# Block maxima by transposing reductions, and the last turn of the mixing beside its product with U

## The chip, the cores and the metric

The kernel runs on one core of a Trainium2 chip. The metric is the device time of one launch in microseconds (us). TensorE (PE) does matrix products and turns (a product with the identity), VectorE (DVE) and ScalarE (ACT) read the products' banks in PSUM, GpSimd (POOL) and SyncE (SP) do the rest. Each engine works through its own queue in order.

## The reference

Three stages on 8 batches, 576 positions, 8 heads of 64 columns:

```python
scores = scale * np.matmul(q, k.transpose(0, 1, 3, 2))
scores = np.where(block_i >= block_j, scores, -1000000000.0)   # blocks of 64
scores = scores - np.max(scores, axis=-1, keepdims=True)
attn = np.exp(scores)
attn = attn / (np.sum(attn, axis=-1, keepdims=True) + 1e-09)
x = np.matmul(attn, v)                       # heads side by side: 576 x 512
...
h = x.transpose(0, 2, 1) @ U @ V             # U: 576 x 32, V: 32 x 576
u = x + h.transpose(0, 2, 1)
x = u + np.maximum(u @ w_ch1, 0.0) @ w_ch2   # 512 -> 2048 -> 512
...
gate = 1.0 / (1.0 + np.exp(-gate_pre))       # causal convolution of 5 steps
out = gate * (x @ w_val) @ w_out
```

## The kernel before

**Stages.** Up to about 240 us PE does the attention of the first two batches (16 heads, "units", queries on the partitions) and the first MLP steps, while 32 conversion steps split the MLP's weights into a high and a low part (DMA, ACT's `magnitude` at L120, four DVE operations at L122 to L143, a cast on ACT). From there to about 1060 us it does the MLP, three products per tile so that a high and a low part together give full precision (`h` at L964, `acc` at L1016), and lays the attention of the other 48 heads between these products. Then come the convolution, the gate and the last two products.

**What sets the order.** PE's order is written by hand: a generator yields pieces of attention and mixing, and the MLP calls `gap()` after a few products, which takes the next piece. What a piece issues on DVE, ACT and POOL is put in its place in their queues by a scheduler, by its own reckoning of when it is ready. In the units (`slot`) the mixing's steps are run to their end with no other PE work within (`for _ in step(pn): pass`). In the late heads (`tick`, `mixing`) each `yield` lets some MLP products in between, six in the places spoken of below.

**Late heads.** Scores of a head lie keys by queries, as five tiles in two halves of 832 and 768 columns (`s`, in places called `za` and `zb`). The softmax's maximum runs over keys, that is over partitions and tiles: `emit_max_a` takes the maximum of the tiles by four operations (L609, L611), `emit_max_b` transposes the result in blocks of 32 by 32 (L618, L619) and takes the maximum in each block's row (L621, 18 columns), and `emit_max_c` joins the four groups of 32 partitions and spreads the result back (`mb`). DVE subtracts it (L647), ACT takes the exponential (L671), PE multiplies by the values (`emit_pv`). `emit_norm_a` turns the row of sums (`lt`) onto the partitions (L745), adds 1e-9 (L747) and takes the reciprocal, and POOL multiplies.

**Mixing.** For each pair of heads (32 pairs: 8 in the units, 24 late) three steps follow each other: `mix_T` turns the head output `xt` in five turns of 128, 128, 128, 128 and 64 positions and splits it into high and low (ACT's cast at L91, DVE's subtraction at L97) in `x`, a buffer that there is once; `mix_G` multiplies by U (five products at L811 into the bank `pG`, 256 columns wide) and adds high and low (L813, L814); `mix_H` multiplies by V (L834) and adds to `xt`. The fifth turn (L803) has a bank of its own. `mix_G` of a pair comes two or more pieces behind its `mix_T`.

**Where the banks come from.** `pT`, `pG`, `pH`, `pPV` and the score pieces take turns in the same pool of PSUM banks (`ps_p`, tag "a"), so a piece that takes one waits for what was last evicted from it.

Of the kernel before, what the change touches and what calls it, by code (L numbers as in the profile page):

```python
# [8 lines left out]
F32 = mybir.dt.float32  # L9
# [4 lines left out]
ALU = mybir.AluOpType  # L14
AX = mybir.AxisListType
PSUM = bass.MemoryType.PSUM
DRAM = bass.MemoryType.DRAM
P = 128
# [4 lines left out]
def attn_moe_gate_kernel(ctx: ExitStack, tc: tile.TileContext, q, k, v, U, V, w1, w2, wval, convw, wout, out):  # L23
# [59 lines left out]
    NB32 = S // 32  # L83

    def f32(ap):
        return ap if ap.dtype == F32 else ap.bitcast(F32)

    vec, act, pool, pe, sp = nc.vector, nc.scalar, nc.gpsimd, nc.tensor, nc.sync

    def hi_act(o, i):  # L90
        act.copy(o, i)  # L91
# [4 lines left out]
    def lo(eng, o, i, h):  # L96
        eng.tensor_tensor(o, i, f32(h), op=ALU.subtract)  # L97
# [9 lines left out]
    def noted(at, ins):  # L107

        mark[at] = ins.ins

    def behind(at):

        return tc.issue_after(mark[at]) if at in mark else nullcontext()
# [77 lines left out]
    def rpool(name, bufs):  # L191
        return att.enter_context(tc.tile_pool(name=name, bufs=bufs, side="right"))
# [8 lines left out]
    tiny_p = rpool("tinyp", 2)  # L201
    ps_p = att.enter_context(tc.tile_pool(name="psp", bufs=ABUF, space=PSUM, side="right"))
# [17 lines left out]
    ident = ac_p.tile([P, P], F32, name="ident")  # L220
# [15 lines left out]
    NTT = (S + P - 1) // P  # L236
    tok = [(P * i, min(P, S - P * i)) for i in range(NTT)]

    def rot(tag, bufs=2, dtype=F32, n=S):
        return rot_p.tile([P, n], dtype, tag=tag, bufs=bufs, name=tag)  # L240
# [46 lines left out]
    NK = NTT  # L287
    q0 = [P * j for j in range(NK)]
    wid = [S - q0[j] for j in range(NK)]
    parts = [(4, 3, 0), (1, 2)]  # L290
    soff, half_of = {}, {}
    sw = []
    for h, js in enumerate(parts):
        o = 0
# [104 lines left out]
    stt = {}  # L399
# [153 lines left out]
    def slot(u):  # L553
# [32 lines left out]
        for step, delay in ((mix_H2, 6), (mix_G, 5), (mix_T, 4)):  # L586
            pn, off = divmod(u - delay, 2)
            if off == 0 and 0 <= pn < 2 * NP:
                with tc.high_priority() if pn == NP - 1 else ExitStack():
                    for _ in step(pn):  # L590
                        pass
                yield False
# [8 lines left out]
    def sv(n, j, a=0):  # L601
        return stt[n][half_of[j]][:, soff[j] + a:soff[j] + wid[j]]

    mbt = {}
    mxt = {}

    def emit_max_a(n):
        m = rot("m", 1)
        vec.tensor_tensor(m[:, P:], sv(n, 0, P), sv(n, 1), op=ALU.max)  # L609
        for j in range(2, NK):  # L610
            x = vec.tensor_tensor(m[:, q0[j]:], m[:, q0[j]:], sv(n, j), op=ALU.max)  # L611
        noted(1, x)
        mxt[n] = m

    def emit_max_b(n):
        m = mxt.pop(n)
        t = rot("t")
        vec.transpose(t[:, 0:P], sv(n, 0)[:, 0:P])  # L618
        vec.transpose(t[:, P:], m[:, P:])  # L619
        r = tiny_p.tile([P, NB32], F32, tag="r0", name="r0")  # L620
        vec.reduce_max(r, t.rearrange("p (j a) -> p j a", a=32), axis=AX.X)  # L621
        mxt[n] = r

    def emit_max_c(n):
# [69 lines left out]
    xts = {}  # L694
# [45 lines left out]

    def emit_norm_a(pn):
        lt = lts.pop(pn)
        t = rot("t")
        with behind(NR0 if pn < NP else 0):
            vec.transpose(t, lt)  # L745
        r = tiny_p.tile([P, NB32], F32, tag="r0", name="r0")
        vec.tensor_scalar(r, t.rearrange("p (j a) -> p j a", a=32)[:, :, 0], 1e-9, None, op0=ALU.add)  # L747
        vec.reciprocal(r, r)
        nrm[pn] = r

# [8 lines left out]
    gst = {}  # L759
# [25 lines left out]
    def mix_T(pn):  # L785
        xt = xts[pn]
        full = S // P
        if not xfix:
            xfix.append(rot("x", 1, F32R, NTT * 2 * P).rearrange("p (i c m) -> p i c m", c=2, m=P))
            pool.memset(f32(xfix[0][tok[-1][1]:, NTT - 1]), 0.0)  # L790
        x = xfix[0]
        gst[pn] = x
        ps = ps_p.tile([P, 512], F32, tag="a", name="pT")
        for i in range(full):
            pe.transpose(ps[:, i * P:(i + 1) * P], xt[:, i * P:(i + 1) * P], ident)  # L795
        pv = ps[:, 0:full * P].rearrange("p (i m) -> p i m", m=P)
        hi_act(x[:, 0:full, 0, :], pv)
        lo(vec, x[:, 0:full, 1, :], pv, x[:, 0:full, 0, :])
        yield
        for i in range(full, NTT):  # L800
            t0, n = tok[i]
            ps = ps_p.tile([P, 512], F32, tag="a", name="pT")
            pe.transpose(ps[:n, 0:P], xt[:, t0:t0 + n], ident)  # L803
            hi_act(x[:n, i, 0, :], ps[:n, 0:P])
            lo(vec, x[:n, i, 1, :], ps[:n, 0:P], x[:n, i, 0, :])

    def mix_G(pn):
        x = gst[pn].rearrange("p i c m -> p i (c m)")
        ps = ps_p.tile([P, 512], F32, tag="a", name="pG")
        for i in range(NTT):  # L810
            pe.matmul(ps[:, 0:2 * P], ust1[:, i, :], x[:, i, :], start=(i == 0), stop=(i == NTT - 1))  # L811
        g32 = rot("t")[:, 0:P]
        act.copy(g32, ps[:, 0:P])  # L813
        vec.tensor_tensor(g32, ps[:, P:2 * P], g32, op=ALU.add)  # L814
        g = rot("g", 4, F32R, P)
        hi_act(g, g32)
        lo(vec, g[2 * R:3 * R], g32[2 * R:3 * R], g[2 * R:3 * R])
        gst[pn] = g
        yield from ()
# [26 lines left out]
    def tick(n, mixed, last=B * NP):  # L846
# [7 lines left out]
        for i in range(4):  # L854
            if new and n % 2 == 0:
                emit_s_piece(n // 2, i)
            if i == (0 if n % 2 else 3) and new:
                emit_corners(n)
                emit_max_a(n)
            yield  # L860
        if new:
            emit_max_b(n)
            if n % 2 == 1:
                prep_t((n + 1) // 2)
# [15 lines left out]
        if old:  # L880
            if e % 2 == 1:
                with tc.high_priority() if URG and e == H - 1 else ExitStack():
                    emit_norm_a(e // 2)
                    emit_norm_b(e // 2)
            yield
        yield from mixing(2 * e + 1, mixed, last)

    def mixing(at, first, last=B * NP):

        for step, delay in ((mix_H2, H0), (mix_G, G0), (mix_T, T0)) if last == NP else ((mix_H2, HPOS), (mix_G, GPOS), (mix_T, TPOS)):  # L890
            pn, off = divmod(at - delay, 4)
            if off == 0 and first <= pn < last:
                if URG and pn == NP - 1:
                    with tc.high_priority():
                        for _ in step(pn):
                            pass
                else:
                    yield from step(pn)
                yield step is mix_H2 and pn % NP == NP - 1
# [391 lines left out]
```

## Time and profile before

| | |
|---|---|
| median of 3 runs | 1446.98 us (1444.05 to 1447.14) |
| profiled execution | 1447.4 us, span 1445.6 us |
| PE busy | 1396.9 us, 97% of the span |
| DVE busy | 1031.9 us, 71% |
| ACT busy | 694.0 us, 48% |
| POOL busy | 320.7 us, 22% |

Busy times are of the whole span. The profile is of one execution. PE's share is an average over stages: it stands mostly in the first 250 us, and hardly at all behind that.

### The profile page before, as it was taken

The numbers are of one execution on the slowest core, as the hardware profiler recorded it, in microseconds if no ns is written. First come the engines' busy times: TensorE is split into PE (matmuls) and PEld (weight loads), VectorE is DVE, ScalarE is ACT, GpSimd is POOL, SyncE is SP. The second block draws the span as 40 slices with busy tenths as digits, with TensorE's granted clock in tenths as the row PEclk, the third lists the DMA queues.
The fourth block names the chain that finished last, engine by engine and source line by source line (L and its number), as shares of the span: only waits on it lengthen the run. The fifth ranks groups of instructions, "written<-read, shape, count | busy, mean of one in ns | idle before, by whom it ended". The sixth has DMA issues, their size and how long they took to land.

```text
span 1445.6 us, 20118 instructions
## 1 busy us (share of the span) xinstructions
PE 1396.9 (97%) x6762; PEld 1086.5 (75%) x6762; DVE 1031.9 (71%) x2113; ACT 694.0 (48%) x1529; POOL 320.7 (22%) x468
## 2 busy tenths in 40 slices
PE   6888878999999999999999999999999999999999
PEld 4666655777777777777777777778888888788887
DVE  6987889588877776888788777776224236499991
ACT  4675544455565555555555555554232211344342
POOL 3543442111121212112111211121031100343310
PEclk9999999999999999999999999999999999999999
DMA  5567766333343334444343433332255433223311
GB/s 110 132 141 209 227 199 164 118 95 85 98 112 87 85 98 112 91 110 120 76 99 85 125 84 87 88 107 82 73 175 175 149 114 117 88 81 102 110 52 66
DMA packets 246289, 163.57 MB, mean 113 GB/s; under 512 B 197669, under 2 KB 212261, under 8 KB 246186
## 3 DMA queue, kind: packets, MB, share of 16 engines
q1 hardware_dynamic: 246186, 162.29, 40.4%
q8 instruction: 54, 0.88, 0.3%
q14 instruction: 49, 0.40, 0.1%
HBM read 134.98 MB, written 27.26 MB: 112 GB/s over the span
## 4 chain that ended last, share of the span: by engine, by line
PE 83%; DVE 6%; DMA 5%; ACT 3%; SPq 1%; issue 1%; POOL 0%; ACTq 0%; DVEq 0%; POOLq 0%
PE h L964 26%; PE acc L1016 25%; PE pPV L735 8%; PE o L1130 7%; PE val L1106 7%; PE pS L413 6%; DMA raw<-in_moe_w_ch_dram 4%; PE pG L811 1%; DVE wa L125 1%; PE acc L1009 1%; PE pS L452 1%; ACT s L467 1%; DVE wa L143 1%; PE pT L795 1%; ACT wa L120 1%
## 5 line engine op out<-in xcount | busy, mean ns | idle before, releaser
L1016 PE MATMUL acc<-hh,w 128*128 128x512 f32 x1152 | 402.1, 402 | 0.0
L1016 PEld LDWEIGHTS acc<-hh,w 128*128 128x128 f32 x1152 | 216.9, 188 | 65.3 <-issue 21.2
L964 PE MATMUL h<-uh,w1hi 128*128 128x512 f32 x576 | 238.3, 414 | 4.9 <-ACT s L418 3.5
L964 PE MATMUL h<-uh,w1lo 128*128 128x512 f32 x576 | 227.4, 395 | 0.0
L964 PE MATMUL h<-ul,w1hi 128*128 128x512 f32 x576 | 226.9, 394 | 0.0
L1016 PE MATMUL acc<-hl,w 128*128 128x512 f32 x576 | 225.6, 392 | 0.0
L993 DVE SCALAR_TENSOR_TENSOR hl<-h,hh 128x512 fp32r<-128x512 f32 x144 | 98.5, 684 | 132.7 <-ACT hh L992 131.5
L992 ACT ACTIVATE hh<-h 128x512 fp32r<-128x512 f32 x144 | 85.9, 597 | 175.6 <-PE h L964 168.7
L964 PEld LDWEIGHTS h<-uh,w1hi 128*128 128x128 f32 x576 | 109.5, 190 | 48.3 <-issue 20.2
L97 POOL TENSOR_TENSOR vlo<-vstk,vhi 128x320 fp32r<-128x320 f32 x46 | 41.8, 908 | 458.3 <-ACT vhi L91 432.0
L964 PEld LDWEIGHTS h<-uh,w1lo 128*128 128x128 f32 x576 | 109.1, 189 | 24.4
L964 PEld LDWEIGHTS h<-ul,w1hi 128*128 128x128 f32 x576 | 109.5, 190 | 18.9 <-issue 0.4
L1016 PEld LDWEIGHTS acc<-hl,w 128*128 128x128 f32 x576 | 108.7, 189 | 19.7 <-issue 0.7
L1088 DVE SCALAR_TENSOR_TENSOR gt<-yb,cw,gt 128x516 f32<-128x516 f32 (+1 forms) x144 | 115.1, 830 | 1.4
L413 PE MATMUL pS<-tq,tk 64*128 64x320 f32 (+4 forms) x576 | 97.7, 430 | 2.4 <-ACT s L418 0.9
L97 POOL TENSOR_TENSOR yl<-yb,yh 128x512 fp32r<-128x512 f32 (+7 forms) x64 | 66.9, 1079 | 107.5 <-ACT yh L91 107.3
L418 ACT COPY s<-pS 128x320 f32<-128x320 f32 (+2 forms) x128 | 60.1, 497 | 50.0 <-PE pS L413 48.8
L97 POOL TENSOR_TENSOR ul<-xt,uh 128x512 fp32r<-128x512 f32 (+7 forms) x64 | 56.1, 883 | 100.8 <-ACT uh L91 100.6
L413 PEld LDWEIGHTS pS<-tq,tk 64*128 64x128 f32 x576 | 44.9, 186 | 39.7 <-issue 23.3
L671 ACT ACTIVATE s<-s 128x448 f32<-128x448 f32 (+1 forms) x62 | 43.8, 711 | 61.5 <-DVE s L647 61.3
L647 DVE TENSOR_TENSOR s<-s,mb 128x64 f32<-128x64 f32 (+4 forms) x160 | 67.3, 483 | 0.3
L97 DVE TENSOR_TENSOR el<-s,eh 128x448 fp32r<-128x448 f32 (+1 forms) x62 | 47.4, 798 | 18.2 <-PE pPV L735 10.6
(187 smaller groups left out, 2684.4 us busy)
## 6 DMA issues: line engine op xcount, KB each, us to landing
w<-w_s SPq DMA_DIRECT2D x144, 512.0 KB, 3.3
rawq<-in_q_dram SPq DMA_DIRECT2D x128, 72.0 KB, 2.7
rawk<-in_k_dram SPq DMA_DIRECT2D x128, 72.0 KB, 3.0
out_dram<-ot SPq DMA_DIRECT2D x35, 256.0 KB, 2.0
vstk<-in_v_dram SPq DMA_DIRECT2D x64, 128.0 KB, 2.5
raw<-in_moe_w_ch_dram SPq DMA_DIRECT2D x64, 128.0 KB, 2.7
raw<-in_moe_w_ch_dram SPq DMA_DIRECT2D x16, 512.0 KB, 4.1
w_s<-wo SPq DMA_DIRECT2D x16, 512.0 KB, 3.7
```

The lines of the kernel that those rows point to most:

```text
L97: eng.tensor_tensor(o, i, f32(h), op=ALU.subtract)
L413: pe.matmul(t[:, o:o + w], tk[me, kslice(j)], tq[me, a0:a1], start=True, stop=True)
L418: act.copy(stt[n][half_of[j]][:, d:d + o], t[:, 0:o])
L647: noted(3, vec.tensor_tensor(sv(n, j), sv(n, j), mb[:, q0[j]:], op=ALU.subtract))
L735: pe.matmul(o_, l_, r_, start=(i == 0), stop=(i == len(todo) - 1))
L964: pe.matmul(ps[:, 0:n], w[:, d, fs], x[:, d, 0:n], start=(d == 0 and i == 0), stop=(d == ND - 1 and i == 2))
L992: act.activation(hh[:, 0:n], ps[:, 0:n], AF.Relu)
L993: latest[0] = vec.scalar_tensor_tensor(hl[:, 0:n], ps[:, 0:n], 0.0, f32(hh[:, 0:n]), op0=ALU.max, op1=ALU.subtract)
L1016: pe.matmul(acc[d][:, 0:n], w[:, wi, ds], x[:, 0:n], start=False, stop=(f == NF - 1 and i == 2))
L1088: vec.scalar_tensor_tensor(gt[d][:, 0:gw], y[:, d, j:j + gw], cw[:, d, j:j + 1], gt[d][:, 0:gw], op0=ALU.mult, op1=ALU.add)
L1106: pe.matmul(ps[:, 0:n], w[:, d, es], x[:, d, 0:n], start=(i == 0), stop=(i == 3 * ND - 1))
L1130: pe.matmul(ps[:m, cs], x[:, e, a:a + m], w[:, e, cs], start=(i == 0), stop=(i == 3 * ND - 1))
```

## The change

Three things change.

1. The late heads' maxima: two `tensor_reduce` with `apply_transpose=True` work directly on the two score halves, transposing 32 by 32 blocks on the way in, and give 26 and 24 columns (one for each 32 queries of each tile). Three joins bring tiles together in place, a fourth with a copy of four columns writes the 18 columns that `emit_max_c` takes over. The buffer `m` and four wide maxima, two transposes and a reduction go.
2. The norm: the transpose and the strided addition become a transposing reduction to 18 columns and an addition on these.
3. The mixing: the fifth turn moves from `mix_T` to the start of `mix_G`, into columns 256 to 383 of `pG`'s own bank. ACT's cast and DVE's low part of it come right behind, then the `yield`, then the five products.

```diff
     def emit_max_a(n):
-        m = rot("m", 1)
-        vec.tensor_tensor(m[:, P:], sv(n, 0, P), sv(n, 1), op=ALU.max)
-        for j in range(2, NK):
-            x = vec.tensor_tensor(m[:, q0[j]:], m[:, q0[j]:], sv(n, j), op=ALU.max)
+        r = tiny_p.tile([P, sum(nblk)], F32, tag="rb", name="rb")
+        for half, (o, w) in enumerate(((0, nblk[0]), (nblk[0], nblk[1]))):
+            x = vec.tensor_reduce(
+                r[:, o:o + w],
+                stt[n][half].rearrange("p (b a) -> p b a", a=BL),
+                axis=AX.X,
+                op=ALU.max,
+                apply_transpose=True,
+            )
...
     def emit_max_b(n):
-        m = mxt.pop(n)
-        t = rot("t")
-        vec.transpose(t[:, 0:P], sv(n, 0)[:, 0:P])
-        vec.transpose(t[:, P:], m[:, P:])
+
+        t = mxt.pop(n)
         r = tiny_p.tile([P, NB32], F32, tag="r0", name="r0")
-        vec.reduce_max(r, t.rearrange("p (j a) -> p j a", a=32), axis=AX.X)
+
+        def join(out, i, j):
+            a, b = t[:, rblk[i]], t[:, rblk[j]]
+            skip = (q0[j] - q0[i]) // BL
+            if out is None:
+                vec.tensor_tensor(a[:, skip:], a[:, skip:], b, op=ALU.max)
+            else:
+                vec.tensor_tensor(out[:, skip:], a[:, skip:], b, op=ALU.max)
+                vec.tensor_copy(out[:, 0:skip], a[:, 0:skip])
+
+        join(None, 1, 2)
+        join(None, 3, 4)
+        join(None, 1, 3)
+        join(r, 0, 1)
...
     def emit_norm_a(pn):
         lt = lts.pop(pn)
-        t = rot("t")
+        r = tiny_p.tile([P, NB32], F32, tag="r0", name="r0")
         with behind(NR0 if pn < NP else 0):
-            vec.transpose(t, lt)
-        r = tiny_p.tile([P, NB32], F32, tag="r0", name="r0")
-        vec.tensor_scalar(r, t.rearrange("p (j a) -> p j a", a=32)[:, :, 0], 1e-9, None, op0=ALU.add)
+            vec.tensor_reduce(r, lt.rearrange("p (b a) -> p b a", a=BL), axis=AX.X, op=ALU.max, apply_transpose=True)
+        vec.tensor_scalar(r, r, 1e-9, None, op0=ALU.add)
...
-        yield
-        for i in range(full, NTT):
-            t0, n = tok[i]
-            ps = ps_p.tile([P, 512], F32, tag="a", name="pT")
-            pe.transpose(ps[:n, 0:P], xt[:, t0:t0 + n], ident)
-            hi_act(x[:n, i, 0, :], ps[:n, 0:P])
-            lo(vec, x[:n, i, 1, :], ps[:n, 0:P], x[:n, i, 0, :])
-
-    def mix_G(pn):
-        x = gst[pn].rearrange("p i c m -> p i (c m)")
-        ps = ps_p.tile([P, 512], F32, tag="a", name="pG")
+        yield from ()
+
+    def mix_G(pn):
+        x4 = gst[pn]
+        ps = ps_p.tile([P, 512], F32, tag="a", name="pG")
+        t0, n = tok[-1]
+        pe.transpose(ps[:n, 2 * P:3 * P], xts[pn][:, t0:t0 + n], ident)
+        hi_act(x4[:n, NTT - 1, 0, :], ps[:n, 2 * P:3 * P])
+        lo(vec, x4[:n, NTT - 1, 1, :], ps[:n, 2 * P:3 * P], x4[:n, NTT - 1, 0, :])
+        yield
+        x = x4.rearrange("p i c m -> p i (c m)")
         for i in range(NTT):
```

The new lines stand 19 or 20 further down: the reductions are L614, the joins L633 to L636, the turn L824, G's products L830, the exponential L691, the subtraction L667, `hh` L1011 and `hl` L1012.

PE at the first `mix_G`, in the units (`pE` are turns of scores, `pS` scores, `x` the split head output, `ust` U), before:

```order
L518 MATMUL pE<-ident,s_163 128x128
L518 MATMUL pE<-ident,s_162 128x128
L811 MATMUL pG<-x,ust_156 128x256 [waits DVE_49]
L811 MATMUL pG<-x,ust_156 128x256 x4
L452 MATMUL pS<-tk,zb 128x512 [waits Activation_49]
L496 MATMUL pPV<-xt,both 128x192 [waits DVE_49,Pool_49]
```

and PE at the same place now:

```order
L518 MATMUL pE<-ident,s_163 128x128
L518 MATMUL pE<-ident,s_162 128x128
L824 MATMUL pG<-ident,xt 64x128 [waits DVE_49,PE_49]
L830 MATMUL pG<-x,ust_156 128x256 [waits DVE_49]
L830 MATMUL pG<-x,ust_156 128x256 x3
L830 MATMUL pG<-x,ust_156 128x256 [waits Activation_49]
L452 MATMUL pS<-tk,zb 128x512
L496 MATMUL pPV<-xt,both 128x192 [waits PE_49,Pool_49]
```

The turn L824 now stands directly ahead of the products, the first product waits for DVE (the low part of that turn), and the fifth for ACT too.

ACT at the late place near 525 us (`hh` is the MLP's evicted first product, `za`, `zb`, `s0`, `s1` the score halves of two heads that the exponential works on), before:

```order
L91 CAST x_570<-pT_5310 128x4x128
L992 ACTIVATE hh_5323<-h1_5303 128x512
L91 CAST x_570<-pT_5327 64x128
L671 ACTIVATE za_5159<-za_5159 128x448
L992 ACTIVATE hh_5368<-h1_5355 128x512
L671 ACTIVATE zb_5160<-zb_5160 128x768
L813 COPY t_5405<-pG_5399 128x128
```

and ACT there now:

```order
L91 CAST x_570<-pT_5268 128x4x128
L1011 ACTIVATE hh_5281<-h1_5261 128x512
L691 ACTIVATE za_5118<-za_5118 128x448
L691 ACTIVATE zb_5119<-zb_5119 128x768
L691 ACTIVATE s0_5120<-s0_5120 128x448
L1011 ACTIVATE hh_5320<-h1_5307 128x512
L691 ACTIVATE s1_5121<-s1_5121 128x768
L91 CAST x_570<-pG_5344 64x128
L832 COPY t_5361<-pG_5344 128x128
```

The cast of the fifth turn moved from ahead of the exponentials to behind four of them, and it now reads `pG`.

DVE at the same place (`mb` is the spread maximum, `hl` the MLP's low part), before:

```order
L993 SCALAR_TENSOR_TENSOR hl_5324<-h1_5303,hh_5323 128x512
L621 TENSOR_REDUCE r0_5383<-t_5380 128x18
L97 TENSOR_TENSOR x_570<-pT_5327,x_570 64x128
L637 COPY r0_5233<-r0_5233 64x18
L627 COPY r1_5411<-r0_5383 64x18
L640 STREAM_TRANSPOSE mb_5261<-r0_5233 128x576
```

and DVE there now:

```order
L660 STREAM_TRANSPOSE mb_5374<-r0_5324 128x576
L667 TENSOR_TENSOR s0_5120<-s0_5120,mb_5374 128x64
L667 TENSOR_TENSOR s0_5120<-s0_5120,mb_5374 128x192
L667 TENSOR_TENSOR s0_5120<-s0_5120,mb_5374 128x576
L667 TENSOR_TENSOR s1_5121<-s1_5121,mb_5374 128x448
L667 TENSOR_TENSOR s1_5121<-s1_5121,mb_5374 128x320
L1012 SCALAR_TENSOR_TENSOR hl_5321<-h1_5307,hh_5320 128x512
L97 TENSOR_TENSOR x_570<-pG_5344,x_570 64x128
L833 TENSOR_TENSOR t_5361<-pG_5344,t_5361 128x128
```

The low part of the fifth turn moved from ahead of both heads' spread maxima and subtractions to behind them.

## Rows read from the trace of the kernel before

**Rows 1.** Stretches: us; busy PE, PEld, DVE, ACT, POOL; PEclk; DMA share; GB/s.

```profile
36.00:240.00 204.00, 173.01 (x974) 124.92 (x973) 172.06 (x351) 114.32 (x303) 82.18 (x92) 0.97 0.68 184
240.00:247.00 7.00, 6.47 (x16) 4.14 (x17) 5.83 (x16) 3.83 (x9) 2.01 (x5) 0.52 0.04 8
247.00:1060.00 813.00, 811.24 (x3972) 629.30 (x3971) 603.26 (x1351) 434.19 (x917) 139.84 (x252) 1.00 0.37 97
```

**Rows 2.** PE's waits to 260 us, then behind: us, times, longest.

```profile
PE pT L803 <- ACT lt L524: 2.9, 4, 1.1
...
PE pT L803 <- ACT lt L737: 0.7, 2, 0.5
```

**Rows 3.** DVE by line, 260 to 1060 us: busy us, mean ns; idle before.

```profile
L611 DVE TENSOR_TENSOR m<-m,s 128x320 f32<-128x320 f32 (+2 forms) x90 | 40.3, 448 | 1.8
...
L621 DVE TENSOR_REDUCE r<-t 128x18 f32<-128x576 f32 x44 | 32.9, 748 | 0.9
L619 DVE STREAM_TRANSPOSE t<-m 128x448 f32<-128x448 f32 x44 | 28.2, 640 | 0.6
...
L745 DVE STREAM_TRANSPOSE t<-lt 128x576 f32<-128x576 f32 x24 | 18.7, 778 | 10.1 <-ACT lt L737 9.3
L609 DVE TENSOR_TENSOR m<-s,s 128x448 f32<-128x448 f32 x30 | 18.0, 600 | 2.6 <-POOL s L598 2.6
...
L747 DVE TENSOR_SCALAR r<-t 128x18 f32<-128x18 f32 x24 | 14.1, 586 | 0.8
...
L618 DVE STREAM_TRANSPOSE t<-s 128x128 f32<-128x128 f32 x30 | 8.8, 292 | 22.9 <-POOL xt L755 11.6 <-POOL s L598 11.2
...
L629 DVE TENSOR_TENSOR r<-r,r 64x18 f32<-64x18 f32 x44 | 6.5, 147 | 0.0
```

**Rows 4.** Timeline of PE, then DVE, 193 to 241 us: start, us, instruction, [idle before].

```profile
193.19 0.75 PE L811 MATMUL pG<-x,ust 128*128 128x256 f32 x5
...
198.87 0.74 PE L834 MATMUL pH<-vst,g 128*128 128x448 f32 x1 [2.20 <-DVE g L97]
...
209.40 0.71 PE L834 MATMUL pH<-vst,g 128*128 128x448 f32 x1 [2.95 <-DVE g L97]
...
240.53 0.79 PE L964 MATMUL h<-uh,w1hi 128*128 128x512 f32 x1 [3.45 <-ACT s L418]
...
199.77 0.69 DVE L125 SCALAR_TENSOR_TENSOR wa<-raw,wa 128x512 uint32<-128x512 uint32 x1
```

**Rows 5.** Timeline of PE, ACT and DVE near 85 us, the third place.

```profile
84.25 0.84 PE L811 MATMUL pG<-x,ust 128*128 128x256 f32 x5
...
85.68 0.88 ACT L524 COPY e<-pE 128x384 f32<-128x384 f32 x2
...
86.84 0.17 DVE L477 RECIPROCAL rq<-rq 128x6 f32<-128x6 f32 x1
```

**Rows 6.** Tile pT, 260 to 700 us: ns min/median/max, first and last start, forms.

```profile
L91 ACT CAST x<-pT x26: 244/421/589, 294.2 to 691.1; 128x512 fp32r<-128x512 f32 x13, 64x128 fp32r<-64x128 f32 x13
```

**Rows 7.** The chain that ended last, 60 to 192 us: start, us, what.

```profile
66.57 5.36 DMA raw<-in_moe_w_ch_dram
...
84.50 0.59 PE pG L811 x5
...
90.33 0.10 SPq L346
```

**Rows 8.** Timeline of PE, ACT and DVE, 508 to 530 us.

```profile
523.55 0.39 PE L964 MATMUL h<-uh,w1lo 128*128 128x512 f32 x1
...
525.14 0.76 PE L811 MATMUL pG<-x,ust 128*128 128x256 f32 x5
...
524.83 0.84 ACT L671 ACTIVATE zb<-zb 128x768 f32<-128x768 f32 x1
...
508.29 0.78 DVE L391 STREAM_TRANSPOSE tq<-rawq 128x576 f32<-128x576 f32 x1 [2.41 <-PE pS L413]
...
527.29 1.95 DVE L647 TENSOR_TENSOR s<-s,mb 128x192 f32<-128x192 f32 x4
```

More of the change, by code (lines that the diff above doesn't have):

```diff
@@ L605, in attn_moe_gate_kernel @@
     mxt = {}
+    BL = 32
+    nblk = [w // BL for w in sw]
+    rblk = [slice(half_of[j] * nblk[0] + soff[j] // BL, half_of[j] * nblk[0] + (soff[j] + wid[j]) // BL) for j in range(NK)]
     def emit_max_a(n):
-        m = rot("m", 1)
-        vec.tensor_tensor(m[:, P:], sv(n, 0, P), sv(n, 1), op=ALU.max)
-        for j in range(2, NK):
-            x = vec.tensor_tensor(m[:, q0[j]:], m[:, q0[j]:], sv(n, j), op=ALU.max)
+        r = tiny_p.tile([P, sum(nblk)], F32, tag="rb", name="rb")
[7 more added lines that the diff above has]
+            )
         noted(1, x)
-        mxt[n] = m
+        mxt[n] = r
     def emit_max_b(n):
-        m = mxt.pop(n)
-        t = rot("t")
-        vec.transpose(t[:, 0:P], sv(n, 0)[:, 0:P])
-        vec.transpose(t[:, P:], m[:, P:])
+        t = mxt.pop(n)
         r = tiny_p.tile([P, NB32], F32, tag="r0", name="r0")
-        vec.reduce_max(r, t.rearrange("p (j a) -> p j a", a=32), axis=AX.X)
+        def join(out, i, j):
[10 more added lines that the diff above has]
+        join(r, 0, 1)
         mxt[n] = r
```

## The prediction

> **What bounds the kernel now.** [...] The wait that the change removes, for a PSUM bank of the mixing's last turn (L803, released by the copy of `lt`), is 2.9 us in 4 waits up to 260 us, and 0.7 us in 2 waits behind it [rows 2]. So there is little to win on PE, and what decides is whether the new order makes PE wait. The timelines of PE, ACT and DVE around the product G (L811) say that. The profiled execution took 1447.4 us; the median of the runs is 1446.98, so the sum is made against 1447.4 and needs no correction.
>
> **Part 1, the late heads' maxima.** One head of today costs DVE 0.600 (L609), three times 0.448 (L611), 0.292 (L618), 0.640 (L619) and 0.748 (L621), in all 3.62 us [rows 3]. Instead come two transposing reductions over 832 and 768 columns. No row shows such an instruction. The transposes of 448 and 576 columns take 640 and 778 ns, so 1.08 ns a column [rows 3]; at one pass the two take about 1.05 and 0.99, in all 2.04 us. If the instruction goes over its data twice, as the transpose and the reduction of 576 columns do now (778 and 748 ns [rows 3]), they take 2.2 and 2.03, in all 4.2 us. To either come four joins and a copy of 2 to 14 columns, at the 147 ns of an 18-column maximum [rows 3] some 0.8 us with the copy. So a head changes from 3.62 to 2.85 us (one pass) or 5.0 us (two). I take one pass, because the 778 ns show a transpose that already streams at the pace of a plain reduction, so one stream suffices for both.
>
> [...]
>
> The maxima lie beside PE's work in all late stages. [...] The most that part 1 can win is thus 6 us, the least nothing; I take -2, as only some of the work ahead of 240 us is maxima.
>
> **Part 2, the norm.** A 576-column transpose (0.778) and a strided operation (0.586) become one transposing reduction and a small operation, about 0.4 us less for each of 24 head pairs [rows 3]. It ends in POOL's multiplication and a turn that PE takes up much later. I take 0.
>
> **Part 3, the bank.** The waits for the turn's own bank go: 2.9 + 0.7 = 3.6 us at most [rows 2]. The early ones stand ahead of other waits, so half is taken: -1.8, bounds 0 and -3.6.
>
> **Part 4, the last turn ahead of G.** This decides. The turn, its ACT copy and DVE's low part stood a whole step ahead of G. Now the order has turn, copy, low part, products in one, and the first product waits for the low part. [...] If only the columns counted, four of the five products could run ahead, which by the 0.84 us of the five [rows 5] would make each wait about half a us shorter; the order as built has the wait on the first, and the sum goes by that.
>
> *Early (8 places, heads of the first two batches).* Nothing stands on PE between turn and products. At the third place G starts at 84.25. ACT's evictions ahead of the copy end at 86.56 (85.68 + 0.88), DVE's reciprocal ahead of the low part ends at 87.01 [rows 5]. A 64-row copy takes 0.244 [rows 6], and the low part is taken at as much, so the copy ends at 86.8, the low part at 87.25 at the latest, and G starts 2.8 to 3.0 late. The other three of the first four read alike. This G is on the chain of work that ended last, up to the load queue at 90.33 [rows 7], so places 3 and 4 are counted in full, 5.7 us. Ahead of place 2 the chain comes over a conversion's DMA [rows 7], and place 1 lies before that; 1 us each, 2 us. Places 5 and 6 (near 132 and 172 us), worked the same way, wait 1.2 and 2.5; half is taken, 2 us. Place 7 starts today at 193.19, but in the new order the copy stands behind a conversion step on ACT, and the low part behind one on DVE that ends at 200.46 [rows 4]: with the low part's own time and without the turn's, 0.27 each, 7.0 us late or less, since the old low part is gone from DVE's queue ahead of it: taken as 6.6. Place 8 is put behind a later conversion step, about 2 us of its own. Of these 8.6 us much is given back, since PE stands 2.20, 2.95 and 3.45 us at the next waits anyway [rows 4]; against that, a PE that stood falls to half clock for a few us, as the stretch from 240 us shows [rows 1]. I take 3. Early sum: 2 + 5.7 + 2 + 3 = 12.7, say +12.7; bounds 0 (all of it falls into later waits) and 24 (all in full).
>
> *Late (24 places).* Between the turn and G now stand six MLP products, about 1.4 us, and then PE waits. The place near 525 us was followed through. The last h product ends at 523.94 (523.55 + 0.39), G starts at 525.14 [rows 8]. In ACT's new order the `hh` activation and a 768-column exponential (0.84 [rows 8]) stand behind that product and ahead of the tail's copy: 523.94 + 0.6 + 0.84 + 0.25, so the copy ends at 525.6 and the low part at 525.9. On DVE the new order puts the next two halves' subtractions ahead of the low part. Today these end at 529.24, with DVE busy without a break since 508.29 [rows 8]. Of that go about 3.2 us (two heads' maxima within the stretch, of which the first reductions move ahead of 508) and 0.5 for the operations of G, so the low part ends at 525.8 to 526.3. G, moved to 525.3 by the turn itself (0.27), is thus 0.5 to 1.0 late. In 15 of the 24 places an exponential stands directly ahead of the copy, in 5 an `hh`, in 4 nothing late. I take 15 x 0.4 + 5 x 0.2 = +7; bounds 0 and, if half a head's delay of DVE hits each place, 24.
>
> Sum: 1447.4 - 2 - 1.8 + 12.7 + 7 = 1463.3, forecast **1463**.
>
> **The rivals.**
> A, the forecast: PE waits at G, with one pass. Its own range is 1453 to 1472.
> B, two passes. DVE's queue is then 1.4 us a head longer than today, and the low part at the place near 525 ends 2.1 us later (two 768-column reductions within the stretch, 1.04 more each). With some 1.5 us more in 15 places the time is 1463 + 22 = 1485. Against it speaks the pace of the transposes; for it, that no row shows the form.
> C, no change: the early waits fall into the 31 us in which PE stands anyway, and late the low part comes before PE has done its six products, because DVE, relieved, runs ahead. That leaves -2 - 1.8 and some 4 of late waits: 1447. For it speaks that DVE and DMA bound the stretch up to 240 us more than PE does; against it, that ACT's order holds the copy behind an exponential, whatever DVE saves.
> D, faster: the relieved DVE removes the wait and the half clock at 240 us, and the early waits are absorbed: 1447.4 - 6 - 1.8 + 1.4 = 1441. It decides if the score evictions at 240 us wait for maxima, and not for the conversion steps.
> E, the change does not do what it says: the built order shows the turn in the bank and the reductions in their places, so this gets no chance of its own.
>
> **How the numbers follow.** A 0.56, B 0.12, C 0.16, D 0.16. A measurement of this kernel tells about 0.2%, 2.9 us, from no change: faster is D, 0.16; same is C, 0.16; slower is A and B, 0.68. The range reaches from within C down towards D and up to near B: 1444 to 1482 leaves out some 0.1 below and 0.08 above. The likeliest case is A with 1463.
>
> **What would show it.** Right: the list of PE's waits has G (the new L830) released by DVE's low part, with some 20 us in up to 32 waits, the longest near 195 us; the transposing reductions over 832 and 768 columns take about 1 us; the bank wait of the turn is gone; behind 260 us PE's idle time grows from about 2 us to about 9. Wrong: reductions of 2 us (B); no row of G among the waits, or stretches up to 247 us that last no longer in spite of it (C); the wait at 240 us gone and the stretch shorter (D). The sum would also be wrong if the new order moved the conversion steps of the first 240 us, whose loads and DVE work PE waits for, by more than the G steps they pass.

## The result: 1.0071 times the time, PE's new waits at G

| | median | ratio to the kernel before, 95% interval |
|---|---|---|
| kernel before | 1446.56 us (1444.05 to 1447.14, 4 runs) | |
| changed kernel | 1456.32 us (1455.81 to 1457.11, 4 runs) | 1.0071 [1.0054, 1.0089] |

The changed kernel is slower by some 10 us; the forecast was 16 us slower, with a range from 1444 to 1482. The waits of PE say where the loss lies. These are lines of the list of waits, first up to 260 us of the profile after, then behind it (total us, times, longest):

```profile
PE pG L830 <- DVE x L97: 19.4, 8, 3.8
...
PE pG L830 <- DVE x L97: 4.6, 6, 1.2
PE pS L413 <- ACT s L418: 1.0, 1, 1.0
PE val L1125 <- DVE gf L1129: 0.8, 1, 0.8
```

All eight early products G wait for the low part of the moved turn, and six of the 24 late ones do. The bank wait of the old turn [rows 2] is gone. The same stretches as in [rows 1] (us; busy PE, PEld, DVE, ACT, POOL; PEclk; DMA share; GB/s):

```profile
36.00:240.00 204.00, 168.30 (x955) 122.45 (x956) 166.31 (x348) 113.98 (x299) 81.04 (x90) 0.97 0.64 181
240.00:247.00 7.00, 6.72 (x25) 3.86 (x26) 7.00 (x16) 4.21 (x8) 0.82 (x4) 1.00 0.25 83
247.00:1060.00 813.00, 807.00 (x3946) 622.25 (x3945) 565.15 (x1349) 435.25 (x917) 138.91 (x253) 1.00 0.37 96
```

From 36 to 240 us PE got through 4.7 us less work than before. From 240 to 247 us it hardly stands (busy for 6.72 of 7.00 us), and its granted clock is 1.00 where it was 0.52. Behind that it is idle for 6.0 us where it was for 1.8, although DVE has 38 us less to do.

How far PE lags at one point is read by setting the same product of both traces side by side. The four score products (64 by 448) ahead of the wait at 240 us start at 236.06 before and at 244.86 now, 8.8 us late; the product with the values that started at 247.12 starts at 249.61, 2.5 us late. The lines of before, then those of after:

```profile
236.06 1.02 PE L413 MATMUL pS<-tq,tk 64*128 64x448 f32 x4
...
247.12 0.38 PE L735 MATMUL pPV<-e,vstk 128*128 128x128 f32 x2
...
244.86 1.02 PE L413 MATMUL pS<-tq,tk 64*128 64x448 f32 x4
245.82 0.50 PE L983 MATMUL h<-uh,w1hi 128*128 128x512 f32 x1
...
249.61 0.38 PE L755 MATMUL pPV<-e,vstk 128*128 128x128 f32 x2
```

So the loss has three parts: +8.8 us up to 236 us, -6.3 us from there to 247 us, and +5.9 us in the late heads. In all that is +8.4, which is what the spans differ by (1454.0 against 1445.6).

DVE by line, 260 to 1070 us of the profile after (busy us, mean ns; idle before):

```profile
L614 DVE TRANSPOSE_TENSOR_REDUCE rb<-s 128x26 f32<-128x832 f32 (+1 forms) x60 | 57.6, 980 | 18.8 <-ACT s L418 16.5 <-POOL s L598 2.3
...
L765 DVE TRANSPOSE_TENSOR_REDUCE r<-lt 128x18 f32<-128x576 f32 x24 | 18.7, 778 | 6.0 <-ACT lt L757 3.5
...
L614 DVE TRANSPOSE_TENSOR_REDUCE rb<-za 128x26 f32<-128x832 f32 x14 | 14.3, 1024 | 5.2 <-ACT za L418 5.1
...
L766 DVE TENSOR_SCALAR r<-r 128x18 f32<-128x18 f32 x24 | 13.9, 581 | 0.8
L614 DVE TRANSPOSE_TENSOR_REDUCE rb<-zb 128x24 f32<-128x768 f32 x14 | 13.1, 935 | 0.0
```

A transposing reduction of 576 columns takes what the transpose of 576 columns took: 778 ns, as L745 did [rows 3]. For 832 and 768 columns it takes 1024 and 935 ns. So at 576 columns the reduction adds nothing to the transpose's 778 ns.

The third early place, near 88 us, of PE, ACT and DVE after (start, us, instruction):

```profile
88.84 0.27 PE L824 MATMUL pG<-ident,xt 128*64 128x128 f32 x1
91.61 0.86 PE L830 MATMUL pG<-x,ust 128*128 128x256 f32 x5 [2.49 <-DVE x L97]
...
90.98 0.26 ACT L91 CAST x<-pG 64x128 fp32r<-64x128 f32 x1
...
91.27 0.28 DVE L97 TENSOR_TENSOR x<-pG,x 64x128 fp32r<-64x128 f32 x1 [0.44 <-ACT x L91]
```

The turn ends at 89.1, but ACT first works off what stands ahead of the cast, as at the same place in [rows 5]. The cast starts at 90.98, the low part at 91.27, G at 91.61.

The late place of [rows 8], on PE, ACT and DVE after:

```profile
527.22 0.27 PE L824 MATMUL pG<-ident,xt 128*64 128x128 f32 x1
...
529.37 0.86 PE L830 MATMUL pG<-x,ust 128*128 128x256 f32 x5 [0.49 <-DVE x L97]
...
527.55 0.58 ACT L1011 ACTIVATE hh<-h 128x512 fp32r<-128x512 f32 x1
528.02 0.83 ACT L691 ACTIVATE s<-s 128x768 f32<-128x768 f32 x1
528.76 0.24 ACT L91 CAST x<-pG 64x128 fp32r<-64x128 f32 x1
...
529.03 0.28 DVE L97 TENSOR_TENSOR x<-pG,x 64x128 fp32r<-64x128 f32 x1 [0.18 <-ACT x L91]
```

The order is `hh`, the exponential of 768 columns, the cast, the low part, G, as it was read from the program, and G waits 0.49 us.

### The profile page after: what moved, and what is told of

Read it like the earlier page. It is cut to its first block, busy times and chain, and to the rows that moved or that the text cites. A ratio compares the mean times of both kernels' runs of the same rounds, so it can differ in the third digit from the quotient of the medians.

```text
span 1454.0 us, 20175 instructions
## 1 busy us (share of the span) xinstructions
PE 1396.5 (96%) x6762; PEld 1083.6 (75%) x6762; DVE 991.9 (68%) x2113; ACT 697.3 (48%) x1529; POOL 318.6 (22%) x468
## 4 chain that ended last, share of the span: by engine, by line
PE 78%; DVE 10%; DMA 5%; ACT 3%; issue 2%; SPq 1%; POOL 0%; ACTq 0%; DVEq 0%; POOLq 0%
PE h L983 24%; PE acc L1035 23%; PE pPV L755 7%; PE o L1149 7%; PE val L1125 6%; PE pS L413 6%; DMA raw<-in_moe_w_ch_dram 4%; PE pG L830 1%; PE acc L1028 1%; DVE wa L125 1%; DVE s L667 1%; DVE wa L143 1%; ACT wa L120 1%; ACT s L467 1%; SPq L947 1%
## 5 line engine op out<-in xcount | busy, mean ns | idle before, releaser
L1012 DVE SCALAR_TENSOR_TENSOR hl<-h,hh 128x512 fp32r<-128x512 f32 x144 | 98.7, 685 | 135.2 <-ACT hh L1011 134.7
L1011 ACT ACTIVATE hh<-h 128x512 fp32r<-128x512 f32 x144 | 85.9, 596 | 176.3 <-PE h L983 171.0
L97 POOL TENSOR_TENSOR ul<-xt,uh 128x512 fp32r<-128x512 f32 (+7 forms) x64 | 52.6, 831 | 119.6 <-ACT uh L91 119.2
L667 DVE TENSOR_TENSOR s<-s,mb 128x64 f32<-128x64 f32 (+4 forms) x160 | 74.7, 529 | 0.6
L614 DVE TRANSPOSE_TENSOR_REDUCE rb<-s 128x26 f32<-128x832 f32 (+1 forms) x64 | 61.5, 981 | 19.0 <-ACT s L418 16.5
```

The lines of the kernel that those rows point to most:

```text
L614: x = vec.tensor_reduce(r[:, o:o + w], stt[n][half].rearrange("p (b a) -> p b a", a=BL), axis=AX.X, op=ALU.max, apply_transpose=True,)
L667: noted(3, vec.tensor_tensor(sv(n, j), sv(n, j), mb[:, q0[j]:], op=ALU.subtract))
L1011: act.activation(hh[:, 0:n], ps[:, 0:n], AF.Relu)
L1012: latest[0] = vec.scalar_tensor_tensor(hl[:, 0:n], ps[:, 0:n], 0.0, f32(hh[:, 0:n]), op0=ALU.max, op1=ALU.subtract)
```

## The experiments

In the results below, "lag" is how far PE is behind (+) or ahead (-) of the kernel before, read at the same product in both profiles as above, at 220, 247 and 1060 us of the kernel before. Behind 1060 us it does not change, unless said.

| kernel | median us | ratio, interval | lag at 220 | at 247 | at 1060 |
|---|---|---|---|---|---|
| changed kernel | 1456.32 | 1.0071 [1.0054, 1.0089] | +9.1 | +2.6 | +8.5 |
| maxima and norm alone | 1447.01 | 0.9993 [0.9984, 1.0003] | +0.7 | -4.2 | -0.1 |
| maxima alone | 1447.00 | 0.9995 [0.9984, 1.0005] | +2.1 | -2.8 | +1.4 |
| mixing alone | 1472.50 | 1.0169 [1.0152, 1.0186] | +13.5 | +10.1 | +26.5 |
| moved turn in the late pairs only | 1449.11 | 1.0010 [0.9997, 1.0023] | -0.8 | -6.7 | -1.0 |
| moved turn in the early pairs only | 1454.37 | 1.0049 [1.0032, 1.0066] | +9.2 | +2.2 | +5.9 |
| a bank of its own for the turn | 1450.69 | 1.0020 [1.0011, 1.0029] | +10.6 | +3.2 | +4.9 |
| exponentials behind the cast | 1453.42 | 1.0036 [1.0022, 1.0050] | +12.6 | +6.2 | +6.1 |
| one more pause ahead of G | 1459.20 | 1.0085 [1.0069, 1.0101] | +11.6 | +5.0 | +7.1 |
| maxima, norm, exponentials behind lt | 1445.18 | 0.9986 [0.9976, 0.9995] | 0.0 | -4.9 | -3.5 |
| before, exponentials behind lt | 1450.93 | 1.0024 [1.0013, 1.0034] | +0.8 | -0.7 | +3.5 |
| mixing alone, exponentials behind the cast | 1471.53 | 1.0169 [1.0155, 1.0182] | +10.0 | +8.1 | +24.3 |
| late turn, exponentials behind its cast | 1442.89 | 0.9965 [0.9951, 0.9979] | +1.8 | -4.0 | -2.3 |

Each ratio is against runs of the kernel before that were taken beside it (the medians of these run from 1446.6 to 1448.7 us), so kernels of different batches are better compared by the ratio than by the median. The lag is that of one profiled execution each. Three of these kernels have the same orders on PE, DVE and ACT as the changed kernel up to the first late pair (the early turn alone, the exponentials behind the cast, the extra pause), and yet their lag at 220 us runs from 9.2 to 12.6. So a lag at 220 us is good to 3 or 4 us, while the difference between two points of one execution is closer: from 220 to 247 us these four give back 6.4 to 7.0.

### Which part brings what

Theory A: the relieved DVE removes the wait at 240 us. Theory B: PE comes later, so that the eviction is ready. Four kernels were to tell them apart.

**Maxima and norm alone.** `mix_T` and `mix_G` are those of the kernel before.

> The maxima and the norm by transposing reductions, the mixing as before. In the changed kernel PE is 9.1 us behind the kernel before at 236 us, and only 2.6 us behind at 247 us: the wait of 3.45 us and the half clock behind it are gone. Theory A: the relieved DVE took them away; then this kernel, in which no G waits, ends at about 1446.6 - 6.5 = 1440. Theory B: PE came 9 us later and the eviction was ready for that reason; then the wait at 240 us stays as it was, and this kernel takes 1445 to 1447. The removed wide maxima save DVE about 0.8 us a head in either.

It took 1447.01 us, no change. In the profile PE is 0.7 us behind at 220 us and 4.2 us ahead at 247 us, so without any delay 4.9 us are given back here. That is most of the size that theory A gave, but not in its way, since the wait at 240 us is still there:

```profile
PE h L983 <- ACT za L418: 2.4, 1, 2.4
```

It is shorter than the 3.45 us of before [rows 4], and the granted clock behind it, up to the product with the values, is 0.68, where it was 0.53. These two make 2.3 of the 4.9 us; the rest comes ahead of 236 us, where among others PE stood 0.86 and 0.50 us for score products and does not now.

The other kernels tell what each side brings to this wait. With the new maxima and no delay it is 2.3 to 2.6 us in all five kernels, and in three of these the clock still falls to 0.68 behind it. With the delay and the old maxima it is 3.1 and 3.3 us. With both it is gone in four kernels of five; in the fifth (the bank of its own) the score products at this place take 1.1 us longer. The clock stays at 1.00 in all five. So neither theory holds alone: the changed kernel loses the wait because DVE is relieved and PE comes late.

Behind 260 us these 4 us are lost again, at a place that the prediction did not name (PE's waits behind 260 us, then the timelines of PE and ACT near 550 us):

```profile
PE pT L822 <- ACT lt L757: 5.5, 5, 1.3
...
552.45 0.30 PE L822 MATMUL pT<-ident,xt 128*64 128x128 f32 x1 [1.29 <-ACT lt L757]
...
547.47 0.58 ACT L691 ACTIVATE s<-s 128x448 f32<-128x448 f32 x1
...
549.33 0.84 ACT L691 ACTIVATE s<-s 128x768 f32<-128x768 f32 x1
...
551.87 0.53 ACT L757 COPY lt<-pPV 64x448 f32<-64x448 f32 x1
```

And ACT at the same place before:

```profile
554.99 0.53 ACT L737 COPY lt<-pPV 64x448 f32<-64x448 f32 x1
...
555.78 1.31 ACT L671 ACTIVATE s<-s 128x448 f32<-128x448 f32 x2
```

With the shorter maxima the scheduler puts the exponentials (448 and 768 columns, 1.4 us) ahead of the copy of `lt`, whose bank the old turn takes over; before they stood behind it. The turn waits 1.1 to 1.3 us in four places, some 134 us apart, and 0.8 in a fifth; before it was 0.7 us in two [rows 2].

**Maxima alone.** The norm stays as it was.

> The maxima alone by transposing reductions; the norm and the mixing as before. Theory: the norm's reduction costs the same 0.78 us as the transpose did and ends off PE's path, so this is the run with both, 1446 to 1448, with PE 4 us earlier at 247 us and the loss behind it for lt. If the norm did something for or against it: off by 2 us or more.

It took 1447.00 us, as with the norm. The norm's edit is worth nothing that can be measured; its small addition still takes 581 ns (L766), where 586 stood before.

**Mixing alone.**

> The last turn ahead of G in G's bank, the maxima and the norm as before. Theory A: the early G waits cost 9 us up to 236 us, nothing is given back at 240 us, and the late ones cost 6 us: 1446.6 + 9 + 6 = 1461 to 1462. Theory B: what is late at 236 us is given back at 240 us, as in the changed kernel: 1446.6 + 2.6 + 6 = 1455.

It took 1472.5 us, far more than either theory gave, and the worst of all. From 220 to 247 us only 3.4 us come back, and the wait at 240 us is still there, although PE comes later than in the changed kernel:

```profile
PE h L964 <- ACT za L418: 3.1, 1, 3.1
```

The late loss is 16.4 us and not 6. The late waits, and one of them, near 540 us, on PE, ACT and DVE:

```profile
PE pG L811 <- DVE x L97: 13.4, 15, 1.7
...
542.21 0.85 PE L811 MATMUL pG<-x,ust 128*128 128x256 f32 x5 [1.67 <-DVE x L97]
...
538.93 0.58 ACT L671 ACTIVATE za<-za 128x448 f32<-128x448 f32 x1 [4.62 <-DVE za L647]
539.87 0.85 ACT L671 ACTIVATE zb<-zb 128x768 f32<-128x768 f32 x1 [0.36 <-DVE zb L647]
540.62 0.58 ACT L992 ACTIVATE hh<-h 128x512 fp32r<-128x512 f32 x1
541.10 0.25 ACT L91 CAST x<-pG 64x128 fp32r<-64x128 f32 x1
...
541.32 0.65 DVE L993 SCALAR_TENSOR_TENSOR hl<-h,hh 128x512 fp32r<-128x512 f32 x1
541.89 0.27 DVE L97 TENSOR_TENSOR x<-pG,x 64x128 fp32r<-64x128 f32 x1
```

With the old maxima the subtraction comes so late that ACT stands 4.62 us for it. Then exponential, exponential, `hh` and cast follow each other. The cast ends at 541.35, but the low part starts only at 541.89, straight behind DVE's own `hl`. G waits in 15 of 24 places. The parts do not add: alone the maxima bring 0 and the mixing +24 to +25 us, together it is +10. Beside the short maxima the moved turn costs less than half of what it costs without them.

**The moved turn in the late or the early pairs only.** A condition in `mix_T` and `mix_G` picks the new or the old form:

```diff
+    def mix_T(pn):
+        yield from (mix_T_new if pn >= 2 * NP else mix_T_old)(pn)
+
+    def mix_G(pn):
+        yield from (mix_G_new if pn >= 2 * NP else mix_G_old)(pn)
```

and for the other kernel `pn < 2 * NP`.

> The changed kernel, but in the first 8 pairs (the units) the last turn is done as before, in its own bank in the step ahead. The first 8 waits of G, 19.4 us, go. Theory A: 1446.6 - 6.5 + 6 = 1446. Theory B: 1446.6 + 6 = 1452.5, since without the delay the wait at 240 us comes back.

> The changed kernel, but in the 24 late pairs the last turn is done as before. The late waits of G, 4.6 us in 6, go; the bank waits of the old turn, 0.7 us, come back. Both theories: PE is some 2.6 us behind at 260 us, and stays so: 1449 to 1450. If the late loss is not due to the turn, 1455.

Late only: 1449.11 us, between the two theories' numbers. By its interval it is no change, and theory B's 1452.5 lies outside. Its profile has PE 0.8 us ahead at 220 us and 6.7 at 247, so 5.9 us come back without any delay, although the wait at 240 us is still 2.6 us long; then 5.7 us are lost late. (The profiled execution, 1446.73 us, is the fastest of eleven, which go up to 1453.83.) Early only: 1454.37 us. Only 2 us of the late loss went with the moved turn, since the old turn then has its own wait, for `lt` as above (4.8 us in 5, in place of G's 4.6 in 6). So with the new maxima's order most of the late loss comes with either turn; that it was due to the moved turn alone, as both theories held, was wrong.

### Why G waits

**A bank of its own.** The turn stays ahead of G, in a tile of its own.

```diff
+        pt = ps_p.tile([P, 512], F32, tag="a", name="pT")
+        pe.transpose(pt[:n, 0:P], xts[pn][:, t0:t0 + n], ident)
...
+        yield
         ps = ps_p.tile([P, 512], F32, tag="a", name="pG")
...
-        pe.transpose(ps[:n, 2 * P:3 * P], xts[pn][:, t0:t0 + n], ident)
```

> The changed kernel, but the moved turn has a PSUM bank of its own beside G's, at the same place. The turn's cast and low part stand where they stood; only the fifth product has to wait for them. If the shared bank makes the first four wait too, each of the 14 places at which G waited gets back up to the time of four products, 0.45 us, some 6 us in all, of which the early half is partly given back elsewhere: 1451 to 1453. If the place of the turn alone decides, and not the bank, 1456 as the changed kernel.

It took 1450.69 us, 5.6 less than the changed kernel (7.4 by the ratios). G's waits (early, then late):

```profile
PE pG L831 <- DVE x L97: 14.2, 9, 2.6
...
PE pG L831 <- DVE x L97: 1.8, 4, 0.7
```

They fall from 24.0 us to 16.0. At the third early place the first four products now run from 88.33, right behind the turn, and only the fifth waits, 2.02 us until 91.07. By the medians more than half of the slowdown is the shared bank, not the place of the turn. The edit also has the turn take a bank of the common pool, so other pieces may get other banks; what that does was not tried apart. In the profiled execution (1452.30 us, above its median) the gain lies late (1.7 us lost behind 247 us, not 5.9); early the lag is not smaller, so what G saves there is waited for elsewhere. In the order as built the first product waits for the low part, although the turn and the products have different columns of the bank, and the run shows what that costs: 19.4 us of early waits against 14.2, and 4.6 of late ones against 1.8. What would happen without the wait no run here shows.

**The exponentials behind the cast.** The mark is the moved turn's cast, and a late head's exponentials that are issued after it are kept behind it:

```diff
-        hi_act(x4[:n, NTT - 1, 0, :], ps[:n, 2 * P:3 * P])
+        act_mark[0] = act.copy(x4[:n, NTT - 1, 0, :], ps[:n, 2 * P:3 * P])
...
         if new:
-            emit_exp(n)
+            with tc.issue_after(act_mark[0].ins) if act_mark[0] else nullcontext():
+                emit_exp(n)
```

> The changed kernel, but ACT's exponentials of a late head are kept behind the cast of the moved turn that was issued ahead of them. Theory A (the exponential ahead of the cast makes G wait late): G's late waits, 4.6 us in 6, fall under 1.5 us, and the time to 1452 to 1453; the 8 early ones stay at 19 us. Rival (DVE's low part is late by its own queue, behind hl): the late waits stay at 4 to 5 us and the time at 1456.

It took 1453.42 us, as this run's theory A has it. The late waits:

```profile
PE pG L832 <- DVE x L97: 0.8, 5, 0.2
```

The late loss is 0.0 (the lag is 6.2 at 247 us and 6.1 at 1060). In the changed kernel it is thus the exponentials in ACT's queue that make G late. In some places they do it by way of DVE: the exponential holds `hh`, and `hl`, which needs `hh`, stands ahead of the low part. `hl` still stands there in this run, and the waits that are left are at most 0.2 us each.

**One more pause.** A second `yield` stands ahead of the products in the late pairs.

> The changed kernel, with one more pause between the moved turn and G in the 24 late pairs, so about twelve MLP products stand between them and not six. If only the cover of 1.4 us is too short, G's late waits, 4.6 us, go nearly to nothing and the time falls to 1451 to 1453. If the copies follow the products in their queues, and not the time, 1456.

It took 1459.20 us, by the medians 2.9 us slower than the changed kernel, though the intervals of the two ratios overlap; it is not faster in any case. PE's waits behind 260 us:

```profile
PE acc L1030 <- ACT y L1049: 2.9, 1, 2.9
PE pG L832 <- DVE x L97: 1.3, 3, 0.6
```

G's late waits fall as forecast, but the stream has one piece more for each pair, the last attention ends later, and PE waits 2.9 us at a point where it did not before, near 1080 us; between 1060 and 1200 us the lag goes from 7.1 to 11.4. More cover between two pieces was not free here, where the pace of the pieces is fixed.

**Mixing alone, exponentials behind the cast.**

> The mixing's change alone with ACT's exponentials kept behind the moved turn's cast. Without that it took 1472 with 13.4 us of late waits of G in 15, and PE lost 16.4 us behind 260 us. If the exponentials ahead of the cast are the cause with the old maxima too, the waits fall under 3 us and the time to 1458 to 1460. If DVE's own queue (the old maxima ahead of the low part) is, most of them stay: 1467 or more.

It took 1471.53 us, so the first expectation failed. The waits stayed. ACT and DVE at one of them, near 537 us:

```profile
PE pG L813 <- DVE x L97: 13.2, 15, 1.7
...
537.98 0.84 ACT L673 ACTIVATE zb<-zb 128x768 f32<-128x768 f32 x1 [0.36 <-DVE zb L647]
538.73 0.58 ACT L995 ACTIVATE hh<-h 128x512 fp32r<-128x512 f32 x1
539.21 0.24 ACT L808 CAST x<-pG 64x128 fp32r<-64x128 f32 x1
...
539.42 0.65 DVE L996 SCALAR_TENSOR_TENSOR hl<-h,hh 128x512 fp32r<-128x512 f32 x1
540.00 0.27 DVE L97 TENSOR_TENSOR x<-pG,x 64x128 fp32r<-64x128 f32 x1
```

The edit moves only exponentials that are issued after the cast. Here it is those of the head ahead that hold `hh` and the cast, and they are late because DVE's subtractions are. So this run does not take away what it set out to. The trace points at DVE's own queue: the cast ends at 539.45, and the low part starts 0.55 us later, straight behind `hl`. That DVE's lateness with the old maxima is the cause is argued from the traces; that these waits are shorter in the changed kernel, with 38 us less on DVE, goes with it.

### Keeping what the maxima bring

**Maxima and norm, exponentials behind `lt`.** The mark is the copy of `lt`, and the exponentials are issued behind the product with the values:

```diff
-        act.copy(lt[own[a], c0:c1], ps[D:P, 0:c1 - c0])
+        act_mark[0] = act.copy(lt[own[a], c0:c1], ps[D:P, 0:c1 - c0])
...
-        if new:
-            emit_exp(n)
         if old:
             emit_pv(e, 1)
+        if new:
+            with tc.issue_after(act_mark[0].ins) if act_mark[0] else nullcontext():
+                emit_exp(n)
```

> The maxima and the norm by transposing reductions, the mixing as before, and ACT's exponentials of a late head kept behind the eviction of lt that the old turn's bank waits for. In the run without that, PE was 4.2 us ahead at 247 us and lost 4.1 behind it, with 5.5 us in 5 waits of the old turn for lt. If the exponentials that a faster DVE lets the scheduler put ahead of that copy are the cause, these waits fall under 1.5 us and the time to 1443. If not, 1447; later exponentials could also make the product with the values wait, then above 1447.

It took 1445.18 us, 0.9986 [0.9976, 0.9995], where 1443 was expected. The wait for `lt` falls from 5.5 us in 5 to one:

```profile
PE pT L824 <- ACT lt L759: 0.8, 1, 0.8
```

The late loss is 1.4 us and not 4.1.

**The same in the kernel before.**

> The kernel before, with only ACT's late exponentials kept behind the eviction of lt. It has 0.7 us of the waits that this takes away late, and nothing of it acts ahead of 240 us. Theory: the gain of the run with the transposing maxima and the kept order comes from the maxima (PE 4 to 6 us earlier at 247 us), so this control takes as long as the kernel before, 1446 to 1447. If the kept order itself is worth the gain: 1444.

It took 1450.93 us: with the old maxima the kept order costs 3 to 4 us, so the gain of the run above is not the order's alone. The waits listed behind 260 us are only 0.7 us more than before. The score products keep PE busy for 3.1 us more from 260 to 1040 us (90.8 against 87.7 us), though one takes as long (428 and 427 ns), so they overlap less; why was not tried.

**Everything together.** Transposing maxima and norm, the old turn in the early pairs, the moved one in the late ones with the exponentials behind its cast.

> Everything that was found put together: transposing maxima and norm, the last turn as before in the 8 early pairs and ahead of G in the 24 late ones, and the exponentials kept behind its cast there. Early as the run with the late turn alone (PE 5 to 6.7 us earlier at 247 us), late as the run with the kept exponentials (nothing lost): 1441 to 1442. If the two do not add, 1445 to 1447.

It took 1442.89 us, 0.9965 [0.9951, 0.9979]: the fastest, and faster than the kernel before by more than the measurement's uncertainty (5 runs, 1440.44 to 1445.33). Late G waits 0.8 us in 5, as in the run with the kept cast; the lag at 1060 us is -2.3 in the profiled execution, which is the slowest of the five.

## Why the prediction was right, and where its terms were off

The forecast was slower by waits of G (case A), with 1463 us; 1456.3 was measured, inside A's own range. Of the 7 us between them, 4 to 5 are what came back at 240 us, and the rest lies mostly in the early waits. By its steps:

- **Part 1, one pass: right.** 1.02 and 0.94 us were measured for 832 and 768 columns, 1.05 and 0.99 were estimated. Rival B (2 us each, 1485 us) is out.
- **Part 1, what it brings at 240 us: mis-sized.** -2 was taken out of 0 to -6. No run shows either term as such: the wait was 3.45 us [rows 4], and the rest of the 6 was the author's estimate for the granted clock of 0.52 behind it [rows 1]. The changed kernel got -6.5 from 220 to 247 us. Ten kernels with the new maxima give back 4.9 to 7.4 there, three with the old ones 1.5 to 3.4. So the maxima themselves are worth 3 to 4 us, the rest comes with PE's delay or with the scatter of executions. The wait itself they only shorten, from 3.5 to some 2.4 us; it goes where PE also comes late, which the prediction, adding its terms one by one, did not reckon with. Rival D left open whether the score eviction waits for maxima or for conversion steps. ACT's queue of the kernel before shows the way:

```profile
239.16 0.90 ACT L681 ACTIVATE e<-za 128x832 f32<-128x832 f32 x1 [5.48 <-DVE za L647]
239.96 0.51 ACT L418 COPY s<-pS 128x448 f32<-128x448 f32 x1
```

  The exponential stands ahead of the eviction and waits 5.48 us for the subtraction, which needs the maximum. DVE's queue ahead of that subtraction, from 225.5 to 238.0 us, is mostly maxima of two heads; one conversion step among them takes 2.1 us.
- **Part 1, nothing in the late stages: wrong.** The prediction let DVE's saving cost and bring nothing there. It costs some 4 us with the old turn as well, because the scheduler now puts exponentials ahead of `lt`; with them kept behind it, 1.4 us are left. That is the step that the prediction had left out: an edit that shortens one engine's work also reorders another's queue.
- **Part 2: a small error without effect.** The addition was to become cheap with a contiguous operand; it takes 581 ns, where 586 stood before.
- **Part 3, the bank waits gone: right** in the changed kernel.
- **Part 4, early: right in kind, a little too large.** 19.4 us of waits in 8 places against the 24 that were worked out; the third place 2.49 against 2.8 to 3.0. The longest, 3.80, is the second place and not the seventh (3.14, where 6.6 was forecast). Behind these two the granted clock was 0.58 (72 to 76 us) and 0.51 (205.7 to 209 us), behind the 2.49 us of the third place 1.00 (91.6 to 95 us). Part of it was given back as forecast: PE's waits ahead of the product with V fall from 5.2 to 1.4 us. Net of that PE was 9.1 us late at 220 us, against 12.7 less the bank's 1.8.
- **Part 4, late: the size right, the sum wrong in its parts.** +7 was forecast, 5.9 measured, which is in part luck. The place near 525 us waits 0.49 us (0.5 to 1.0 forecast), but only 6 places wait at all, 4.6 us in all; the moved turn accounts for some 2 us of the loss by the run with the early turn alone, since the wait for `lt` takes its place there.
- **Rivals C and D** named the right thing with the wrong result. Part of the early loss was indeed given back at 240 us, and there the wait and the slow clock were gone (1.00 where 0.52 stood), as D has it, though not by the relieved DVE alone. The early waits were not absorbed by what followed, as C had it with its 31 us (204.00 less 173.01 [rows 1]). The change without the moved turn takes as long as C's 1447, by another way.

## What to carry to other kernels

Before a step is moved next to the product that needs it, look at what stands between in the queues of the engines that carry it over: here a cast of 0.25 us and the low part behind it cost 0.4 to 3.8 us in 14 of 32 places, because they stood behind evictions, exponentials and `hl`. In the shared bank the readers of one half held back the writer of the other, and a bank of its own was worth 5.6 us. And a shorter operation changed the order that the scheduler chose for the engines behind it; the gain was kept when the one copy that PE waits for was held in its place.

A change of two parts can also do something that neither does alone: the wait at 240 us goes with the relieved DVE and the late PE together, while the relieved DVE alone takes some 1 us of it and the late PE alone 0.2 to 0.4.

## What was not expected of the hardware

A reduction with a transpose on the way in took as long as the transpose alone (778 ns for 576 columns either way). An 18-column addition of a constant takes 581 ns, and 586 with a strided operand, while the reciprocal of the same 18 columns takes 262; why was not tried. Executions with the same order early on differ by 3 to 4 us in where PE stands at 220 us. And the same wait does not always bring the same clock: behind 2.3 to 2.6 us of waiting at 240 us the granted clock was 0.68 in three kernels and 1.00 in two, which is some 1.5 us of time.
